# Windowed attention with a squared-ReLU layer: batch 0 started as 512 tokens, v cast by its own load, q and k ahead of v, and one transpose moved to the DMA

## The chip, the core and the metric

The kernel runs on one core of a Trainium2 chip. The metric is the device time of one execution in microseconds (us); the number given for the kernel before is the median of eight runs. The profile is of one execution. Engines: PE multiplies matrices, ACT evaluates functions, DVE and POOL work elementwise, SP only issues DMAs here. POOL issues DMAs too[...]. Each engine works through its own list of instructions in order.

## What is computed

Four batches of 768 tokens with 8 heads of 64. Each token attends to the first 4 tokens (the sinks) and to the 128 tokens up to itself; the output, one row of 512 a token, goes through two dense layers with a squared ReLU between them.

```python
scores = scale * np.matmul(q, k.transpose(0, 1, 3, 2))       # 4 x 8 x 768 x 768
keep = (pos[None, :] < 4) | ((rel >= 0) & (rel < 128))
scores = np.where(keep, scores, -1e9)
a = exp(scores - max); a = a / sum(a)
x = (a @ v), heads side by side                               # 3072 x 512
h = np.maximum(x @ w_in, 0); out = (h * h) @ w_out            # 512 -> 2048 -> 512
```

## The kernel before

**Tiling.** A batch is six tiles of 128 tokens, handled in three parts of 256 tokens, s = 0, 1, 2. Heads go in four pairs, m = 0 to 3. For one part and one pair: `scores` (L563) multiplies keys by queries into PSUM (tile `ps`), `expo` (L597) is the exponential on ACT (tile `expm`), a mask follows (`domask`, L604; in batch 0 a bias is instead added on PE by matmuls at L573 and the mask falls away), `values` (L624) multiplies by v for two pairs at a time (tile `po`), and `norm` (L648) divides on DVE into `xn_sb`. The sink keys have a small matmul of their own (`pk`) and exponential (`es`). `bridge` (L673) turns x by eight PE transposes (tile `px`), and `bridge_copy` (L684) brings it from PSUM to `xT`. For batches 2 and 3 (NATURAL) the turns of q, k and x are DMA transposes from SP instead (L434, L664). `layer1` (L691) multiplies 16 blocks of w_in by xT into `pm`, squares the ReLU with ACT and DVE; `layer2` (L722) multiplies by w_out into `py`.

**Loading.** For batches 0 and 1 q and k come as f32 (`load_qk`, L323, tile `qr`), are cast and regrouped on DVE, POOL or ACT (`regroup`, L451, tile `qs`), turned on PE (`transpose`, L468, tile `pt`) and copied from PSUM (`unload`, L486, tile `qkT`). A row that lies together in HBM is 64 f32 values times the number of tokens a partition takes: 512 B for groups of 256 tokens, 1 KB for groups of 512. v comes as f32 in rows of 256 B (`load_v`, L352, tile `vf`) and is cast by DVE or POOL (`cast`, L506). Batches 2 and 3 load q, k and v through POOL's queue, which casts (`load_natural`, L366). The weights are loaded and cast through POOL's queue too, in eight DMAs (`load_w_in`, `load_w_out`, L296 to L310).

**Order.** `Plan` (L41) is a planner that runs when the program is built: every piece of work is an `op` with a key (its wish for a place), the engines that can do it with a cost in us, what it comes after, the PSUM buffers it takes (two in the pool `att`, two in `den`), and for DMAs a queue. It always takes the op that can start first, and so fixes each engine's order. PE_SLACK (L18), the `margin` of DMAs and the fractions at L813 to L849 only steer this choice. `behind` makes a DMA's issue wait for an earlier DMA to land; `warm` (L196) puts matmuls without use into expected pauses of PE.

**The start.** The lines L784 to L811 give the order of the loads. Batch 0 is three groups of 256 tokens (L319). SP loads q and k of group 0, then half of group 1, v of part 0, the other half, v of part 1. The first w_in load waits for the k load of group 1's second half (L794); the first q k load of the last group waits for the first w_out load, and batch 1's q k for the third.

Of the kernel before, what the change touches and what calls it, by code (L numbers as in the profile page):

```python
# [17 lines left out]
PE_SLACK = 0.219  # L18
# [115 lines left out]
def kernel(  # L134
# [28 lines left out]
    sizes = dict(att=2, den=2, qr=5, qs=6, vf=3, expm=8, r=3, osb=2)  # L163
# [149 lines left out]
    qr_slot, qs_slot, vf_slot = {}, {}, {}  # L313
    qn_t, qn_slot = {}, {}
    qr_t, qs_t, vf_t, ex_t, bank_t = {}, {}, {}, {}, {}
# [3 lines left out]
    GROUPS[0] = [(0, 2), (256, 2), (512, 2)]  # L319
# [3 lines left out]
    def load_qk(b, m0, ti, g, behind=None, yields=()):  # L323


        t0, n = GROUPS[b][g]
        if b == 0 and g < 2:
            half, share = g, (b, m0, ti)
        elif n == 2:
            half, share = m0 // 2, (b, "last", ti)  # L330
        else:
            half, share = None, (b, m0, ti)
        if not half:
            qr_slot[share] = Slot("qr", 2)
        qr_slot[b, m0, ti, g] = qr_slot[share]

        def run(e):
            if half is not None:
                if half == 0:
                    qr_t[share] = work["qr"].tile([128, 2, 4, n * D], FP32, name="qr", tag="qr")  # L340
                t = qr_t[share][:, half]
            else:
                t = work["qr"].tile([128, 4, n * D], FP32, name="qr", tag="qr")
            qr_t[b, m0, ti, g] = t
            return [nc.sync.dma_start(  # L345
                out=t,
                in_=(q, k)[ti][b, 2 * m0:2 * m0 + 4, t0:t0 + 128 * n, :].rearrange(
                    "h (p t) d -> p h (t d)", t=n))]
        ops["qk", b, m0, ti, g] = dma_op("sp", ("qk", b, m0, ti, g), run, 32 * ROW[256 * n], behind,
                                         () if half else [qr_slot[share]], yields)  # L350

    def load_v(b, s, behind=None, yields=()):  # L352

        sl = vf_slot[b, s] = Slot("vf", 1)
        for i in range(2):
            t = 2 * s + i

            def run(e, i=i, t=t):
                if i == 0:
                    vf_t[b, s] = work["vf"].tile([128, 2, H, D], FP32, name="vf", tag="vf")  # L360
                return [nc.sync.dma_start(  # L361
                    out=vf_t[b, s][:, i], in_=v[b, :, 128 * t:128 * t + 128, :].rearrange("h p d -> p h d"))]
            dma_op("sp", ("v", b, t), run, 8 * 8 * ROW[256], behind if i == 0 else None,
                   [sl] if i == 0 else (), yields)

    def load_natural(b, s, older_values):  # L366

        begun = [ops["layer1", b - 2, 0, 0], w_out_op[3]]
        for ti in (1, 0):
            if s == 0:  # L370
                qn_slot[b, ti] = Slot("qr", NT)
            for i in range(2):
                t = 2 * s + i

                def run(e, t=t, ti=ti):
                    if t == 0:
                        qn_t[b, ti] = work["qr"].tile([128, NT, DM], BF16, name="qn", tag="qr")
                    return [nc.gpsimd.dma_start(  # L378
                        out=qn_t[b, ti][:, t, :].rearrange("p (h d) -> p h d", d=D),
                        in_=(q, k)[ti][b, :, 128 * t:128 * t + 128, :].rearrange("h p d -> p h d"))]  # L380
                o = dma_op("pool", ("qk", b, ti, t), run, 64 * 0.032,
                           ("v", 1, 3) if (b, ti, t) == (2, 1, 0) else None,
                           [qn_slot[b, ti]] if t == 0 else ())
                o.after += begun
                o.margin = 2.229
        for t in (2 * s, 2 * s + 1):
            def run(e, t=t):
                return [nc.gpsimd.dma_start(  # L388
                    out=v_sb[b % 2][:, t, :, 0:D],
                    in_=v[b, :, 128 * t:128 * t + 128, :].rearrange("h p d -> p h d"))]  # L390
            o = dma_op("pool", ("v", b, t), run, 64 * 0.032)
            o.after += begun + older_values
            o.margin = 2.229
# [6 lines left out]
    def attention(b, key):  # L400
# [16 lines left out]
        def stage(g, f0, f1, side):  # L417
# [9 lines left out]
            if b in NATURAL:  # L427
                for s in range(NS):
                    for ti in (1, 0):
                        for i in range(2):  # L430
# [8 lines left out]
                            ops["turn", b, ti, t].margin = 4.81  # L439
# [3 lines left out]
            for m in range(0, NP, w) if b not in NATURAL else ():  # L443
                f = 0.08 * m
                m0 = m - m % 2
                bs = Slot(side, 2)
                regs = []
                for ti in (1, 0):
                    sl = qs_slot[b, m, ti, g] = Slot("qs", 1)

                    def regroup(e, m=m, m0=m0, ti=ti):  # L451
                        t = qs_t[b, m, ti, g] = work["qs"].tile([128, w, n, 2, D], BF16, name="qs", tag="qs")
                        r = qr_t[b, m0, ti, g][:, 2 * (m - m0):2 * (m - m0) + 2 * w, :]
                        if w == 2:
                            copy(e, t, r.rearrange("p (m h) (t d) -> p m t h d", m=2, d=D))
                        else:
                            copy(e, t[:, 0], r.rearrange("p h (t d) -> p t h d", d=D))
                    who = {"pool": 0.17 + w * n * 0.11}
                    if b or g < 2:
                        who["dve"] = 0.06 + w * n * 0.094  # L460
                    if b == 0 and g == 0:
                        who["act"] = 0.2 + w * n * 0.107
                    regs.append(op(at(f), who, regroup,
                                   after=[ops["qk", b, m0, ti, g]] + prev_tr + begun, takes=[sl],
                                   reads=[qr_slot[b, m0, ti, g]]))
# [38 lines left out]

            for s in range(t0 // 256, last // 256) if b not in NATURAL else ():
                def cast(e, s=s):  # L506
                    copy(e, vb[:, 2 * s:2 * s + 2, :, 0:D], vf_t.pop((b, s)))
                ops["cast", b, s] = op(at(0.3 + 0.5 * (256 * s - t0) / (last - t0)),
                                       {"pool": 1.08, "dve": 0.75} if g < 2 else {"pool": 1.08}, cast,
                                       after=[ops["v", b, 2 * s], ops["v", b, 2 * s + 1], c_sinks] + older_values + begun,  # L510
                                       reads=[vf_slot[b, s]])


            if g == 0:
# [7 lines left out]
                def sink_values(e):  # L522
                    for j in range(NP):
# [5 lines left out]
                A["sink_values"] = op(at(0.36), {"pool": 1.4, "dve": 0.9}, sink_values,  # L529
                                      after=older_values + [c_fill, c_sinks, ops["vs_in", b]])  # L530
# [23 lines left out]
            biased = b == 0 and g < 2  # L554
            for s in range(t0 // 256, last // 256):
                fs = 0.36 + 0.5 * (256 * s - t0) / (last - t0)
                norms = []
                for m0 in (0, 2):
# [4 lines left out]
                    def scores(e, ms, s=s, m0=m0, banks=banks):  # L563
# [32 lines left out]
                    for j, m in enumerate((m0, m0 + 1)):  # L596
# [19 lines left out]
                        if biased:  # L616
                            masked.append(ex)
                            continue
                        masked.append(op(at(fm + 0.03), {"pool": 1.3, "dve": 0.7} if s else {"dve": 0.58, "pool": 1.1},
                                         domask, after=[ex, late["masks"]]))  # L620
# [40 lines left out]
                if b in NATURAL:  # L661
                    for t in (2 * s, 2 * s + 1):
# [5 lines left out]
                        o_.margin = 3.168  # L668
# [115 lines left out]
    NATURAL = (2, 3)  # L784
    load_sinks("act", 0)
    for g, m0 in ((0, 0), (0, 2), (1, 0), (1, 2)):
        for ti in (1, 0):
            load_qk(0, m0, ti, g)
        if g:
            load_v(0, m0 // 2)  # L790
    for b in range(1, B):
        load_sinks("sp", b)
    for i in range(4):
        load_w_in(i, ("qk", 0, 2, 1, 1) if i == 0 else None)  # L794
    load_w_out(0)
    load_w_out(1)
    for m0 in (0, 2):
        for ti in (1, 0):
            load_qk(0, m0, ti, 2, ("w_out", 0) if m0 == 0 and ti == 1 else None, [("w_out", 1)])
    load_v(0, 2, None, ())  # L800
    load_w_out(2, ("v", 0, 4), [("v", 0, 5)])
    load_w_out(3, None, ())
    for m0 in (0, 2):
        for ti in (1, 0):
            load_qk(1, m0, ti, 0, ("w_out", 2) if m0 == 0 and ti == 1 else None, [("w_out", 3)])
    for m0 in (0, 2):
        for ti in (1, 0):
            load_qk(1, m0, ti, 1, None, ())
    load_v(1, 0, None, ())
# [3 lines left out]
    LO, HI = 0.03, 0.504  # L813
    for b in range(B):
        if b == 0:
            at = attention(0, lambda f: f - 1.0)
            at(0, 0.0, 0.5, ("den", "att"))
            at(1, 0.5, 1.0, ("den", "att"))
            w_in_op[2].follow += [ops["cast", 0, 0]]
            w_out_op[0].follow += [ops["cast", 0, 1]]  # L820
            late["masks"] = op(-0.029, {"pool": 3.0}, build_masks, after=[c_tri, ops["bridge", 0, 1]])
            at(2, 1.0, 0.869, ("att", "den"))
# [4 lines left out]
        else:  # L827
            for i, fb in enumerate(range(0, NFB, 2)):
                layer1(b, b + 0.306 * i / 8, (fb, fb + 1), 0, 512, (0, 1))
        for i, fb in enumerate(range(0, NFB, 4)):  # L830
            if b == 0:
                layer1(b, 0.225 + 0.179 * i / 4, range(fb, fb + 4), 512, 256, (2,))
            else:
                layer1(b, b + 0.306 + 0.167 * i / 4, range(fb, fb + 4), 512, 256, (2,))
        if b + 1 < B:
# [3 lines left out]
            if b == 0:  # L839
                at = attention(1, lambda f: f)  # L840
                at(0, 0.063, 1.0, ("att", "den"))
                at(1, 0.249, 0.449, ("att", "den"))
            else:
                attention(b + 1, lambda f, b=b: b + LO + (HI - LO) * f)(0, 0.0, 1.0, "att")
        for u in range(NS):
            if b == 0 and u < 2:
                layer2(b, u, lambda i, part, u=u: 0.403 + 0.303 * (4 * part + 2 * u + i) / 24, by_part=True)
# [38 lines left out]
```

The softmax here doesn't subtract the row's maximum and nothing guards it: scores larger than these inputs give would overflow.

## Time and profile before

| | us |
|---|---|
| median of 8 runs | 226.07 (225.93 to 226.33) |
| the profiled execution | 226.17 |
| its span in the profile | 224.5 |
| first matmul of the first dense layer | 18.76 |
| PE busy | 215.7 |
| ACT busy | 115.3 |
| DVE busy | 103.5 |
| POOL busy | 63.5 |

The span is the time from the first to the last instruction; 1.67 us of the execution lie around it. The page gives the busy time of each engine, the span in 40 slices of 5.6 us, and the chain of work that ended last, followed back from the end. PE's warm-up matmuls count as busy. Up to 18.76 us PE works on batch 0's attention alone; then the dense layers of each batch run with the attention of the next between them, and the last 41 us have nothing but batch 3's dense layers.

### The profile page before, as it was taken

To read this page: it belongs to the slowest core of one execution; us is meant where nothing else is said; L and a number is where in the kernel's file an instruction comes from. 1 tells how busy PE (TensorE), PEld (TensorE's weight loads), DVE (VectorE), ACT (ScalarE), POOL (GpSimd) and SP (SyncE) were. 2 spreads that over 40 slices of the span, in tenths; PEclk is the share of its full clock that TensorE was granted. 3 is DMA by queue.
4 is the path that set the end of the run, shared out by engine and by line. 5 is a ranking of instruction groups with operands and counts; after the bars stand their busy time and mean duration, and the time that the engine had idled before them with its cause. 6 is when DMAs were issued, how large, how long until landed. Compare 5 with 4: busy or idle time off the path is not lost.

```text
span 224.5 us, 4571 instructions
## 1 busy us (share of the span) xinstructions
PE 215.7 (96%) x1919; PEld 137.9 (61%) x1941; DVE 103.5 (46%) x190; ACT 115.3 (51%) x130; POOL 63.5 (28%) x97
## 2 busy tenths in 40 slices
PE   7989999999999999999999999999999999999993
PEld 7557996457865796555454555587464555884441
DVE  7573534456775577446372533456344123440010
ACT  2486365517776587287636276665443066551010
POOL 5179016134389935987200000000002000000000
PEclk9999999999999999999999999999999999999999
DMA  5999996999999999999999552000121430000222
GB/s 168 264 192 205 213 227 148 187 354 274 214 240 160 125 204 131 163 129 200 153 129 136 147 152 58 3 0 14 36 103 26 133 120 0 0 0 3 93 95 93
DMA packets 86357, 29.70 MB, mean 132 GB/s; under 512 B 70336, under 2 KB 82880, under 8 KB 86336
## 3 DMA queue, kind: packets, MB, share of 16 engines
q0 software_dynamic: 40128, 8.92, 50.6%
q1 hardware_dynamic: 46024, 20.35, 39.6%
q8 instruction: 15, 0.25, 0.5%
q10 hardware_dynamic: 184, 0.14, 0.2%
q14 instruction: 6, 0.05, 0.1%
HBM read 27.30 MB, written 6.29 MB: 150 GB/s over the span
## 4 chain that ended last, share of the span: by engine, by line
PE 87%; DMA 5%; SPq 3%; ACT 2%; issue 1%; DVE 1%; ACTq 0%
PE pm L701 38%; PE py L741 37%; PE po L641 6%; PE ps L580 4%; DMA w_in_sb<-in_moe_w_in_dram 3%; DMA qr<-in_k_dram 2%; ACT r L710 2%; SPq L345 1%; SPq L361 1%; PE pt L477 1%; PE px L678 1%; PE pk L540 0%; DVE qkT L208 0%; ACT qkT L206 0%; DVE osb L208 0%
## 5 line engine op out<-in xcount | busy, mean ns | idle before, releaser
L701 PE MATMUL pm<-xT,w_in_sb 128*128 128x256 bf16 (+1 forms) x576 | 87.0, 308 | 1.1 <-ACT r L710 0.6
L741 PE MATMUL py<-w_out_sb,gT 128*128 128x512 bf16 x364 | 86.6, 379 | 1.2 <-issue 0.2
L701 PEld LDWEIGHTS <-w_in_sb 128*128 128x128 bf16 x576 | 62.9, 114 | 21.8 <-issue 2.1
L710 ACT ACTIVATE r<-pm 128x1024 bf16<-128x1024 f32 x48 | 49.2, 1026 | 33.7 <-PE pm L701 27.2
L741 PEld LDWEIGHTS <-gT 128*128 128x128 bf16 x384 | 35.4, 98 | 38.5 <-issue 1.4
L599 ACT ACTIVATE expm<-ps 128x1024 bf16<-128x1024 f32 (+1 forms) x48 | 43.3, 953 | 22.6 <-PE ps L580 21.4
L717 DVE TENSOR_TENSOR gT<-r 128x1024 bf16<-128x1024 bf16 x48 | 33.2, 691 | 44.5 <-ACT r L710 44.5
L608 DVE TENSOR_TENSOR expm<-expm,mask 128x1024 bf16<-128x1024 bf16 (+1 forms) x37 | 24.6, 671 | 16.6 <-ACT expm L599 16.0
L206 ACT ACTIVATE osb<-py 128x1024 f32<-128x1024 f32 x10 | 10.3, 1027 | 25.1 <-PE py L741 18.0
L222 POOL TENSOR_SCALAR_AFFINE_SELECT expm<-expm 128x512 bf16<-128x512 bf16 x4 | 2.5, 638 | 68.4 <-ACT expm L599 62.7
L641 PEld LDWEIGHTS <-expm 128*128 128x128 bf16 x352 | 16.6, 97 | 4.9 <-issue 0.8
L641 PE MATMUL po<-v,expm 128*128 128x65 bf16 x352 | 17.9, 193 | 0.3 <-DVE v L208 0.2
L653 DVE TENSOR_TENSOR xn_sb<-po,rc 128x512 bf16<-128x512 f32 x24 | 16.6, 691 | 0.8
L652 DVE RECIPROCAL rc<-po 128x8 f32<-128x8 f32 x24 | 5.0, 206 | 24.4 <-PE po L641 24.0
L580 PE MATMUL ps<-qkT 64*128 64x128 bf16 (+1 forms) x256 | 14.7, 238 | 0.4
L580 PEld LDWEIGHTS <-qkT 64*128 64x128 bf16 x256 | 8.1, 94 | 10.3 <-issue 8.9
L641 PE MATMUL po<-vs,es 128*128 128x65 bf16 x128 | 13.1, 193 | 0.0
L210 POOL CAST qs<-qr 128x512 bf16<-128x512 f32 x11 | 7.9, 732 | 18.2 <-DMA qr<-in_k_dram 11.8
L208 DVE COPY osb<-py 128x1024 f32<-128x1024 f32 (+2 forms) x3 | 2.3, 780 | 21.0 <-PE py L741 17.9
L641 PEld LDWEIGHTS <-es 128*128 128x128 bf16 x128 | 11.7, 97 | 0.0
L378 POOL DMA_DIRECT2D qn<-in_k_dram x12 | 10.8, 910 | 2.7 <-DMA vf<-in_v_dram 2.7
L388 POOL DMA_DIRECT2D v<-in_v_dram x12 | 10.7, 898 | 2.8 <-DMA qn<-in_q_dram 2.4
(51 smaller groups left out, 113.1 us busy)
## 6 DMA issues: line engine op xcount, KB each, us to landing
out_dram<-osb SPq DMA_DIRECT2D x11, 512.0 KB, 3.2
vf<-in_v_dram SPq DMA_DIRECT2D x12, 256.0 KB, 5.6
qr<-in_k_dram SPq DMA_DIRECT2D x8, 256.0 KB, 4.9
qr<-in_q_dram SPq DMA_DIRECT2D x8, 256.0 KB, 4.4
w_in_sb<-in_moe_w_in_dram POOLq DMA_DIRECT2D x4, 512.0 KB, 8.6
w_out_sb<-in_moe_w_out_dram POOLq DMA_DIRECT2D x4, 512.0 KB, 9.3
qn<-in_k_dram POOLq DMA_DIRECT2D x12, 128.0 KB, 7.4
qn<-in_q_dram POOLq DMA_DIRECT2D x12, 128.0 KB, 9.0
```

The source lines that it names most:

```text
L206: nc.scalar.activation(out=dst, in_=src, func=AF.Copy)
L378: return [nc.gpsimd.dma_start(out=qn_t[b, ti][:, t, :].rearrange("p (h d) -> p h d", d=D), in_=(q, k)[ti][b, :, 128 * t:128 * t + 128, :]. ...
L388: return [nc.gpsimd.dma_start(out=v_sb[b % 2][:, t, :, 0:D], in_=v[b, :, 128 * t:128 * t + 128, :].rearrange("h p d -> p h d"))]
L580: nc.tensor.matmul(ps[:, h2, o:o + w], lhsT=qkT_sb[r, m, 1, c, :], rhs=qkT_sb[r, m, 0, qb:qb + w // 128, :], start=(i == 0 and not biased) ...
L599: nc.scalar.activation(out=x[:, :, o:512], in_=bank_t["s", b, s, m][:, :, o:512], func=AF.Exp, scale=scale)
L608: nc.vector.tensor_mul(x[:, :, o:512], x[:, :, o:512], mk[:, :, o:512])
L641: nc.tensor.matmul(pv[:, i, h2, :], lhsT=lhsT, rhs=rhs, start=(n_ == 0), stop=(n_ == len(mms) - 1))
L653: nc.vector.tensor_tensor(out=xn_sb[:, 2 * s:2 * s + 2, 128 * m0:128 * m0 + 256].rearrange("p i (j h d) -> p j i h d", j=2, d=D), in0=pv[: ...
L701: nc.tensor.matmul(pm[:, i, :], lhsT=w_in_sb[:, fb // 4, kb, fb % 4:512:4], rhs=xT[:, c0 // 256:(c0 + cw) // 256, kb, :], start=(kb == 0), ...
L710: nc.scalar.activation(out=r, in_=bank_t.pop(tag), func=AF.Relu)
L717: (nc.vector if e == "dve" else nc.gpsimd).tensor_mul(gT_sb[c0 // 512][:, fbs[0]:fbs[0] + n, c0 % 512:c0 % 512 + cw], r, r)
L741: nc.tensor.matmul(pm[:, i, :], lhsT=gT_sb[t // 4][:, fb, 128 * (t % 4):128 * (t % 4) + 128], rhs=w_out_sb[:, fb, :], start=(fb == 0), sto ...
```

## The change

Batch 0 becomes a group of 512 tokens and one of 256, so that its first eight q k loads take one pair of heads each, in rows of 1 KB. In this first group the key copy and the query copy of a pair are two copies, and each pair's scores need both. v of batches 0 and 1 is loaded by POOL's queue straight into `v_sb`, cast on the way: the tile `vf`, the casts on DVE and POOL and SP's twelve v loads are gone. All eight q k loads of batch 0's first group stand ahead of everything else on SP; POOL issues four v loads and the sink values of batch 0 before w_in, and w_in's first load now waits for the k load of pair 2. Batch 1's q k wait for the last v load of batch 0, and batch 1's v for its own k load of pairs 2 and 3 of the last group. Part 2 of batch 1 is turned by two DMA transposes on SP (`TURNED`) instead of eight PE transposes and a PSUM copy. The fractions, margins and PE_SLACK have other values. Both parts of batch 0's first group keep the bias on PE (BIASED = 2).

```diff
-PE_SLACK = 0.219
+PE_SLACK = 0.292
...
-    sizes = dict(att=2, den=2, qr=5, qs=6, vf=3, expm=8, r=3, osb=2)
+    sizes = dict(att=2, den=2, qr=5, qs=6, expm=8, r=3, osb=2)
...
-    GROUPS[0] = [(0, 2), (256, 2), (512, 2)]
+    GROUPS[0] = [(0, 4), (512, 2)]
...
-        if b == 0 and g < 2:
-            half, share = g, (b, m0, ti)
-        elif n == 2:
+        if n == 2:
             half, share = m0 // 2, (b, "last", ti)
+        elif pairs == 1:
+            half, share = m0 % 2, (b, m0 - m0 % 2, ti)
...
             return [nc.sync.dma_start(
                 out=t,
-                in_=(q, k)[ti][b, 2 * m0:2 * m0 + 4, t0:t0 + 128 * n, :].rearrange(
+                in_=(q, k)[ti][b, 2 * m0:2 * m0 + 2 * pairs, t0:t0 + 128 * n, :].rearrange(
                     "h (p t) d -> p h (t d)", t=n))]
...
-                return [nc.sync.dma_start(
-                    out=vf_t[b, s][:, i], in_=v[b, :, 128 * t:128 * t + 128, :].rearrange("h p d -> p h d"))]
-            dma_op("sp", ("v", b, t), run, 8 * 8 * ROW[256], behind if i == 0 else None,
-                   [sl] if i == 0 else (), yields)
+                return [nc.gpsimd.dma_start(
+                    out=v_sb[b % 2][:, t, :, 0:D],
+                    in_=v[b, :, 128 * t:128 * t + 128, :].rearrange("h p d -> p h d"))]
+            o = dma_op("pool", ("v", b, t), run, 1.15, behind if t == 2 * s else None, (), yields)
+            o.after.append(c_fill)
+        ops["cast", b, s] = o
...
-                def cast(e, s=s):
-                    copy(e, vb[:, 2 * s:2 * s + 2, :, 0:D], vf_t.pop((b, s)))
...
-                A["sink_values"] = op(at(0.36), {"pool": 1.4, "dve": 0.9}, sink_values,
-                                      after=older_values + [c_fill, c_sinks, ops["vs_in", b]])
+                A["sink_values"] = op(at(0.36), {"pool": 1.9, "dve": 1.4} if b else {"pool": 1.9}, sink_values,
+                                      after=older_values + [c_fill, c_sinks, ops["vs_in", b]] +
+                                      ([ops["bridge", 0, 1]] if b == 1 else []))
...
-                if b in NATURAL:
+                if b in NATURAL or b == 1 and s in TURNED:
                     for t in (2 * s, 2 * s + 1):
                         def turn_x(e, t=t):
                             nc.sync.dma_start_transpose(out=xT[:, t // 2, :, 128 * (t % 2):128 * (t % 2) + 128],
                                                         in_=xn_sb[:, t, :])
...
-    for g, m0 in ((0, 0), (0, 2), (1, 0), (1, 2)):
+    for m in range(NP):
         for ti in (1, 0):
-            load_qk(0, m0, ti, g)
-        if g:
-            load_v(0, m0 // 2)
+            load_qk(0, m, ti, 0, 1)
     for b in range(1, B):
         load_sinks("sp", b)
+    load_v(0, 0, None)
+    load_v(0, 1)
     for i in range(4):
-        load_w_in(i, ("qk", 0, 2, 1, 1) if i == 0 else None)
+        load_w_in(i, ("qk", 0, 2, 1, 0) if i == 0 else None)
...
+    load_w_out(2, ("qk", 0, 2, 1, 1), [("qk", 0, 2, 0, 1)])
     load_v(0, 2, None, ())
-    load_w_out(2, ("v", 0, 4), [("v", 0, 5)])
     load_w_out(3, None, ())
     for m0 in (0, 2):
         for ti in (1, 0):
-            load_qk(1, m0, ti, 0, ("w_out", 2) if m0 == 0 and ti == 1 else None, [("w_out", 3)])
+            load_qk(1, m0, ti, 0, 2, ("v", 0, 5) if m0 == 0 and ti == 1 else None, [("w_out", 3)])
...
-    load_v(1, 0, None, ())
+    load_v(1, 0, ("qk", 1, 2, 1, 1), [("qk", 1, 2, 0, 1)])
...
-            at(0, 0.0, 0.5, ("den", "att"))
-            at(1, 0.5, 1.0, ("den", "att"))
-            w_in_op[2].follow += [ops["cast", 0, 0]]
-            w_out_op[0].follow += [ops["cast", 0, 1]]
-            late["masks"] = op(-0.029, {"pool": 3.0}, build_masks, after=[c_tri, ops["bridge", 0, 1]])
-            at(2, 1.0, 0.869, ("att", "den"))
+            at(0, 0.0, 1.0, ("den", "att"))
+            late["masks"] = op(0.04, {"pool": 3.0}, build_masks, after=[c_tri, ops["bridge", 0, 1]])
+            at(1, 0.928, 1.5, ("att", "den"))
...
-                at(0, 0.063, 1.0, ("att", "den"))
-                at(1, 0.249, 0.449, ("att", "den"))
+                at(0, 0.072, 0.526, ("att", "den"))
+                at(1, 0.975, 0.471, "att")
```

## The prediction

> **What bounds the kernel now.** I read the page's busy times and slices first, then the chain of waits in order of time, then busy times by window, then single waits in the timeline. The page:
>
> ```profile
> PE 215.7 (96%) x1919; PEld 137.9 (61%) x1941; DVE 103.5 (46%) x190; ACT 115.3 (51%) x130; POOL 63.5 (28%) x97
> PE   7989999999999999999999999999999999999993
> DMA  5999996999999999999999552000121430000222
> ```
>
> PE is the bound, and no change to another engine pays unless PE starts its dense work earlier or idles less. The DMA row is full over the first 30 us, so the start may still hang on loads. The chain of waits over the start says which (start, us, what):
>
> ```profile
> 7.10 5.29 DMA qr<-in_k_dram
> 12.39 0.30 issue
> 12.69 6.03 DMA w_in_sb<-in_moe_w_in_dram
> 18.72 0.05 issue
> 18.76 1.94 PE pm L701 x16
> 20.70 1.45 PE po L641 x48
> 22.15 1.75 PE pm L701 x16
> 23.90 0.45 PE px L678 x8
> 24.35 10.48 PE pm L701 x96
> ```
>
> A late k load (issued at 7.10 because SP first had to push v) lets w_in go at 12.69; w_in lands at 18.72 and PE's dense work begins. At that point batch 0's second part is not finished: 48 `po` (1.45 us) and 8 `px` (0.45) come after. The fair mark is therefore 18.76 + 1.45 + 0.45 = 20.66 us: from there on only dense work and what lies between it remain. The changed order has no dense matmul before both parts are turned; its first `pm` stands behind the second `px`. Its start X compares with 20.66.
>
> Busy time by window (us, then PE, PEld, DVE, ACT, POOL, clock, DMA share, GB/s) shows what idling is left after the start:
>
> ```profile
> 34.83:54.35 19.52, 19.10 (x178) 10.68 (x181) 10.32 (x19) 9.61 (x12) 8.19 (x13) 1.00 0.94 243
> 54.35:75.55 21.20, 20.42 (x235) 15.20 (x236) 13.02 (x23) 14.43 (x19) 15.10 (x18) 1.00 1.73 192
> 75.55:93.67 18.12, 17.80 (x216) 13.61 (x217) 12.39 (x24) 12.36 (x14) 12.10 (x17) 1.00 1.86 167
> ```
>
> PE idles 0.42, 0.78 and 0.32 us there, and some 0.5 us in all later windows: 2.0 us is all that a better order can win after the start. The timeline names the two real stalls, first dense layer waiting for its PSUM buffer:
>
> ```profile
> 59.91 1.91 PE L701 MATMUL pm<-xT,w_in_sb 128*128 128x256 bf16 x16 [0.28 <-ACT r L710]
> 62.92 1.91 PE L701 MATMUL pm<-xT,w_in_sb 128*128 128x256 bf16 x16 [0.34 <-ACT r L710]
> ```
>
> [...] 214 GB/s with 256 B rows (56 to 60 us), 272 with 512 B (2 to 4 us), 363 with 1 KB (46 to 50 us). [...] the trace has both queues at once at 69 to 72 us with a DMA share of 2.29. [...] the chain has 0.45 for 8 `px`.
>
> **Part 1, the loads of the start.** The first 256 KB k load lands 3.0 us after its issue, at 3.8, and the second 0.85 later. With 1 KB rows I take 0.78 a load (256 KB in 0.72 us at 363 GB/s, between that and 0.85): k q of pair 0 land at about 3.7 and 4.5, pair 1 at 5.3 and 6.1. POOL finishes its constants at 4.11 and then issues four v loads of 0.89 (L388). Their packets arrive from about 6 us and share with the last three q k loads. Free sharing gives pair 3's q at 9.2, strict addition (four times 0.9 us, the spacing of landings of the `qn` loads) 12.8. I take 9.9, as most of v's small packets can fit beside q k; k of pair 3 then lands at 9.0. In the kernel before the last q of this stage lands at 13.3 (issued 8.76, 4.5 to land). v itself lands by 11 to 13, needed at 13 and 17: hidden. After v POOL does the sink values (2.16 us as at 15.85 now) and issues w_in at about 9.9, against 12.69. Its 6.0 us shrink or stay: w_in lands at 15 to 16, no longer on the path.
>
> **Part 2, the front as ACT sees it.** With loads early, the front is ACT's list. Prices: 0.60 for a 512-wide `qkT` copy on ACT, 0.69 on DVE, 0.43 for a cast on DVE, 0.81 for an exponential over 768, 1.03 over 1024, 0.39 for `es`; an ACT cast is not in the trace, between 0.43 and 0.69, I take 0.62. PE runs 40 warm-up matmuls until 5.7, as now, so the first `pt` ends and ACT starts at 6.86, as now. ACT must then do, before the last exponential ends, three copies 1.80, two casts 1.24, four exponentials over 768 3.24, four over 1024 4.12, `es` 0.39: 10.8 us, to 17.7 at best. Waits inside: 0.3 for pair 3's k (9.0), 0.15 because DVE does pair 3's first copy only after two of pair 2 and one late cast, some 0.1 of handovers: 18.3. After it 24 `po` (0.73, to 19.1), DVE's reciprocal and division (0.21 + 0.69, to 20.0), 8 `px` behind 10 warm-ups (to 20.5), and the copy of the first part's `xT`, which ends about 20.6. X = 20.6, bounds 20.1 (no ACT waits) and 22 (q k at 12.8: pair 3's cast and copy 2.5 later, part of it filled by earlier exponentials). Against 20.66: **-0.06 us**. The front is not shortened, because an ACT-bound wait takes the place of the DMA-bound one and no dense matmul fills it. DVE's and POOL's saved v casts lie beside it: nothing.
>
> **Part 3, the moved transpose.** Eight PE transposes go: **-0.45 us** of PE. Their PSUM copy of 1.0 us on ACT goes too, beside PE's work. Two DMA transposes come to SP, 1.23 us each to issue (L664), 2.5 to 8.3 to land. They stand behind the turns of batch 2's last third and before batch 3's first; in PE's new list 26 us of work lie between these `po` and the first `pm` of part 2, so a landing even 10 us late is hidden. Batch 3's turns behind them wait at most for DVE's division, long before their readers.
>
> **Part 4, loads for the body.** Everything behind w_in moves forward by about 2.5 to 3 us: before, w_out's first load is issued at 17.95, lands 11.3 later, and batch 0's last q k start at 29.25. Counting forward with the same gaps, batch 0's last q k land at 31 to 34, with PE reaching their first `pt` at X + 12.1 = 32.7 (112 `pm` of 0.108); part 2's v by 40, needed at 41.7; batch 1's first q by 46, cast by 47, needed at 47.9. Each margin is 0.7 to 1.2 us. The six v loads of batch 1 cost POOL 5.3 us, against 2.1 for its casts on POOL now; they follow batch 1's q k (about 52) and land from 57, with values at 60. Batch 2's loads start near 58 rather than 62.5. So hidden, if w_in's packets start by 12.5; each us after that costs nearly one, once, as all three margins slip together.
>
> **Part 5, PE's stalls in the body.** Counting PE, ACT and DVE through 46 to 65 us in the new order with these prices, I find no wait of a first-layer matmul for its buffer: fewer `pt` sit between them, and the second layer's first accumulator is copied out by ACT 0.7 us before it is wanted. The two stalls (0.28 + 0.34) can go; bounds: all 1.5 of the three windows gained, 1.5 lost in a new order this tight. I take **-0.4**.
>
> Sum against the profiled execution: 226.17 - 0.06 - 0.45 - 0.4 = 225.26; it stands 0.10 above the median of 226.07. Forecast **225.2**.
>
> **Rivals.** (a) Slower: v in the start. The mechanism is POOL's v packets inside the q k stream. If v's packets don't fit beside them, pair 3 lands near 12 and w_in's packets start at 13 to 14. It decides from pair 3's k later than 10 us. X becomes about 21.5 and the margins of part 4 go under by about 1: 225.26 + 0.9 + 1.0 = 227.1 (226.5 to 228). For it: one queue alone already shows a DMA share of 1.24 (w_in at 20 to 24 us), so little may be free; against it: 2.29 at 69 to 72. (b) No change: the front comes a few tenths later and the new body trades its stalls for others, leaving only the transposes or less: 225.7 to 226.5, say 226.1. For it: the closest margin that I count, batch 1's first scores after DVE's last copy of their keys, is under 0.1 us, and there are 170 more groups of work that I did not count through. (c) Faster by more: ACT never waits in the front (X = 20.1) and the body loses 1 us of idling: 226.17 - 0.5 - 0.45 - 1.0 = 224.2. Against: it needs every margin. That the change doesn't do what it says is excluded: the order shows v on POOL's queue and one PSUM turn less.
>
> **How the numbers follow.** A measurement here tells 0.2% (0.45 us) from no change. Forecast (224.6 to 225.6) 0.38, (c) 0.10, (b) 0.20, (a) and other new stalls of its size 0.32. Faster 0.48, same 0.20, slower 0.32. The forecast's own range is 224.6 to 225.6; the range that leaves out no more than 2 in 10 runs from 224.3 to 227.3.
>
> **What would show it.** Right: the first `pm` at 20 to 21 us and waiting for `xT` or `px`, never for w_in; ACT busy without a gap over 0.4 us from 6.9 to 18.3; w_in's wait for a load gone from the chain; `pm` without stalls at 55 to 65. Wrong: ACT or DVE waiting for `qr` after 9.5 us; PE waiting for `qs` near 33 or 48 us, or for v at 42; any wait of `pm` for the DMA-turned `xT`.

## The result and the profile after

| | before | after |
|---|---|---|
| median, us | 226.15 (225.75 to 226.58) | 228.73 (226.91 to 230.41) |
| ratio after to before | | 1.0111, interval 1.0092 to 1.0129 |
| the profiled execution, its span | 226.17, 224.46 | 230.38, 228.7 |
| first `pm` | 18.76 (mark 20.66) | 21.57 |
| PE's last matmul | 220.81 | 224.26 |
| from there to the end of the span | 3.65 | 4.41 |

The changed kernel is slower by 2.6 us, and its executions spread over 3.5 us where the kernel before spreads over 0.8. The profiled one is among the three of twelve with a mean TensorE clock of 0.988 to 0.991; the others had 0.995 or more, so what a half clock costs in the profile is not in the median. The ratios, here and below, leave out executions that are over 1.5% above the fastest of their kernel, and the median above leaves out the profiled one.

The page of the changed kernel, busy times and two of the rows of slices:

```profile
PE 217.1 (95%) x1923; PEld 138.0 (60%) x1943; DVE 103.3 (45%) x193; ACT 115.2 (50%) x131; POOL 63.3 (28%) x97
PE   7699999999699999999999999999999999999992
...
PEclk9999999999979999999999999999999999999998
```

PE has 0.45 us of matmuls less to do, yet is busy 1.4 us longer. One slice at 57 to 63 us has a 6 in PE's row; the next one has a 7 in the clock's. Busy time by window (us, then PE, PEld, DVE, ACT, POOL, clock, DMA share, GB/s) around it:

```profile
60.00:62.90 2.90, 1.15 (x13) 0.74 (x12) 1.52 (x3) 1.43 (x3) 2.68 (x4) 1.00 2.32 151
62.90:67.10 4.20, 4.20 (x31) 3.21 (x31) 1.50 (x3) 0.64 (x1) 3.51 (x4) 0.59 2.21 213
```

PE loses 1.75 us in the first window and works at a mean clock of 0.59 in the second. The timeline of PE names the wait, and the chain of waits (start, us, what) follows it back:

```profile
60.91 0.24 PE L634 MATMUL po<-v,expm 128*128 128x65 bf16 x2
62.90 0.46 PE L634 MATMUL po<-v,expm 128*128 128x65 bf16 x10 [1.76 <-DMA v<-in_v_dram]
63.20 5.00 PE L694 MATMUL pm<-xT,w_in_sb 128*128 128x256 bf16 x29
```

```profile
46.28 0.68 DVE qs L208 x2
46.96 0.02 issue
46.98 0.37 SPq L348
47.35 0.05 issue
47.40 6.41 DMA qr<-in_k_dram
53.80 0.02 issue
53.83 0.02 POOLq L361
53.84 0.87 issue
54.71 0.95 POOL v L361
55.66 7.20 DMA v<-in_v_dram
```

Batch 1's v is late. SP's last q k loads wait for a `qr` buffer until DVE has cast it (46.96), POOL's first v load waits for the gate, the k load that lands at 53.80, then 0.87 us go by before its issue begins. The second tile of v lands at 62.86, when the first two `po` have run and PE stands. The clock is at half from 63.67 us, just after the pause, to 67.09, and 32 `pm` take 5.2 us instead of about 3.5 (estimated from 10.48 us for 96 in the kernel before). The two stalls at 59.9 and 62.9 in the kernel before are gone.

The start, in the timelines of DVE, first of the kernel before, then of the changed one:

```profile
6.34 0.43 DVE L208 CAST qs<-qr 128x512 bf16<-128x512 f32 x1 [0.39 <-DMA qr<-in_k_dram]
9.15 0.43 DVE L208 CAST qs<-qr 128x512 bf16<-128x512 f32 x1 [0.53 <-DMA qr<-in_q_dram]
```

```profile
6.16 0.43 DVE L208 CAST qs<-qr 128x512 bf16<-128x512 f32 x1 [1.44 <-DMA qr<-in_k_dram]
8.04 0.63 DVE L208 CAST qs<-qr 128x512 bf16<-128x512 f32 x1 [1.45 <-DMA qr<-in_q_dram]
```

Now DVE waits 2.9 us for the k and q of pair 1, PE waits behind it 1.68 us before it can turn pair 1's q, and the first `pm` comes at 21.57. In the kernel before the third and the fourth load landed at 6.32 and 7.27 us, here at about 6.1 and 8.02: hardly faster there, but w_in's landing at 18.72 stood after them and hid it.

Against the profiled execution of before, +4.2 us: start +0.9, wait for v +1.8, half clock +1.7, end +0.75, and about -1.0 for transposes and stalls that went.

### The profile page after: what moved, and what is told of

It reads as the page before. It is cut to its first block, busy times and chain, and to the rows that moved or that the text cites. A ratio compares the mean times of both kernels' runs of the same rounds, so it can differ in the third digit from the quotient of the medians.

```text
span 228.7 us, 4568 instructions
## 1 busy us (share of the span) xinstructions
PE 217.1 (95%) x1923; PEld 138.0 (60%) x1943; DVE 103.3 (45%) x193; ACT 115.2 (50%) x131; POOL 63.3 (28%) x97
## 4 chain that ended last, share of the span: by engine, by line
PE 81%; DMA 9%; DVE 2%; ACT 2%; SPq 2%; issue 1%; POOL 0%; DVEq 0%; POOLq 0%; ACTq 0%
PE pm L694 36%; PE py L734 32%; PE po L634 6%; PE ps L571 4%; DMA v<-in_v_dram 3%; DMA qr<-in_q_dram 3%; DMA qr<-in_k_dram 3%; SPq L348 2%; DVE qkT L208 1%; ACT r L703 1%; PE px L671 1%; PE pt L476 1%; ACT qkT L206 1%; PE ps L564 1%; PE pk L531 0%
## 5 line engine op out<-in xcount | busy, mean ns | idle before, releaser
L694 PE MATMUL pm<-xT,w_in_sb 128*128 128x256 bf16 (+1 forms) x576 | 88.7, 313 | 0.3 <-DVE xT L208 0.2
L599 DVE TENSOR_TENSOR expm<-expm,mask 128x1024 bf16<-128x1024 bf16 (+1 forms) x39 | 25.1, 649 | 18.6 <-ACT expm L590 18.0
L206 ACT ACTIVATE osb<-py 128x1024 f32<-128x1024 f32 x9 | 9.2, 1027 | 34.6 <-PE py L734 33.6
L222 POOL TENSOR_SCALAR_AFFINE_SELECT expm<-expm 128x512 bf16<-128x512 bf16 x2 | 1.2, 637 | 55.8 <-ACT expm L590 55.8
L571 PEld LDWEIGHTS <-qkT 64*128 64x128 bf16 x256 | 8.0, 94 | 10.1 <-issue 8.0
L208 DVE COPY osb<-py 128x1024 f32<-128x1024 f32 (+2 forms) x4 | 3.6, 890 | 21.3 <-PE py L734 18.2
L208 DVE CAST qs<-qr 128x512 bf16<-128x512 f32 x18 | 8.7, 493 | 7.5 <-DMA qr<-in_q_dram 4.0
L361 POOL DMA_DIRECT2D v<-in_v_dram x12 | 10.8, 918 | 2.7 <-DMA qr<-in_k_dram 2.7
L390 POOL DMA_DIRECT2D v<-in_v_dram x12 | 10.8, 911 | 2.2 <-DMA qn<-in_q_dram 2.0
```

The costliest lines, as they stand in the source:

```text
L206: nc.scalar.activation(out=dst, in_=src, func=AF.Copy)
L208: nc.vector.tensor_copy(out=dst, in_=src)
L361: return [nc.gpsimd.dma_start(out=v_sb[b % 2][:, t, :, 0:D], in_=v[b, :, 128 * t:128 * t + 128, :].rearrange("h p d -> p h d"))]
L571: nc.tensor.matmul(ps[:, h2, o:o + w], lhsT=qkT_sb[r, m, 1, c, :], rhs=qkT_sb[r, m, 0, qb:qb + w // 128, :], start=(i == 0 and not biased) ...
L599: nc.vector.tensor_mul(x[:, :, o:512], x[:, :, o:512], mk[:, :, o:512])
L694: nc.tensor.matmul(pm[:, i, :], lhsT=w_in_sb[:, fb // 4, kb, fb % 4:512:4], rhs=xT[:, c0 // 256:(c0 + cw) // 256, kb, :], start=(kb == 0), ...
```

## Experiments

In all of them, the time from the first `pm` to PE's last matmul is read beside the median, because the start varies from run to run. The kernel before has 200.15 us from its mark of 20.66, and 202.05 from its own first `pm`, with which the last three rows compare; the prediction comes to 200.15 - 0.45 - 0.4 = 199.3. There is one profile for each kernel.

| kernel | median (before, same chip) | ratio, interval | first `pm` | `pm` to last matmul | to the end |
|---|---|---|---|---|---|
| after | 228.73 (226.15) | 1.0111, 1.0092-1.0129 | 21.57 | 202.69 | 4.41 |
| v ungated | 226.71 (226.22) | 1.0024, 1.0008-1.0039 | 20.67 | 199.84 | 4.54 |
| v gated earlier | 227.26 (226.35) | 1.0038, 1.0025-1.0051 | 22.26 | 199.11 | 4.63 |
| matmuls in the pause | 228.47 (226.22) | 1.0102, 1.0080-1.0124 | 20.97 | 201.16 | 4.60 |
| v ungated, v of batch 0 behind q | one execution: 229.92 | | 21.26 | 202.37 | 4.60 |
| v ungated, turn on PE | 227.11 (226.35) | 1.0033, 1.0018-1.0049 | 21.59 | 200.24 | 3.91 |
| v ungated, SP filled, 12 | 226.39 (226.35) | 1.0002, 0.9984-1.0020 | 20.97 | 199.11 | 3.52 |
| the same, 24 | 226.41 (226.49) | 1.0003, 0.9992-1.0014 | 21.13 | 199.48 | 3.89 |
| the same, two queues | 226.54 (226.49) | 1.0009, 0.9995-1.0023 | 22.12 | 199.11 | 3.81 |
| before with the DMA turn | 232.54 (226.22) | 1.0245, 1.0183-1.0307 | 19.52 | 209.24 | 3.52 |
| the same, margin 6.5 | 232.62 (226.29) | 1.0271, 1.0234-1.0307 | 18.81 | 209.69 | 3.54 |
| the same, margin 8 | 233.94 (226.29) | 1.0334, 1.0310-1.0357 | 18.89 | 209.50 | 3.56 |

**The gate of batch 1's v.** First without it, every engine's order unchanged:

```diff
-            if behind is not None:
+            if behind is not None and name[:2] != ("v", 1):
```

> Changed kernel, but batch 1's v loads no longer wait for a k load to land; every instruction of every engine keeps its place. Theory V (the changed kernel loses its time because batch 1's v lands late: PE idles 1.8 us at 61 us and then runs 3.4 us at half clock): v is issued at about 52 right after POOL's last q cast, lands by 60, the 1.76 us wait of po and the half clock after it are gone, the time is 226.5 (226.0 to 227.0) and its runs spread less than 1 us. Theory F (the front costs it all, and the wait for v only takes up slack that PE would lose anyway): the wait goes, another takes its place, the time stays within 0.7 us of 228.7. Theory C (v issued earlier takes DMA time from batch 1's last q k): v lands no earlier than 61 and PE waits for qs or v as long as now.

PE runs through, in its timeline, at the place of the pause:

```profile
60.74 0.54 PE L634 MATMUL po<-v,expm 128*128 128x65 bf16 x12
61.12 3.11 PE L694 MATMUL pm<-xT,w_in_sb 128*128 128x256 bf16 x27
```

The clock stays at 1.00, and the median falls to 0.5 us above the kernel before; the executions spread over 1.5 us, where under 1 was expected. Then with an earlier gate:

```diff
-                    after_dma(d, loaded[behind])
+                    after_dma(d, loaded[("qk", 1, 0, 1, 1) if name[:2] == ("v", 1) else behind])
```

> The changed kernel, with batch 1's v loads gated on the first of the last four q k loads (landed at 52.1 in the changed kernel's trace) in place of the third (53.8). Theory V (PE waits at 61 us because v is issued too late): v lands 1.6 to 1.7 us earlier, the wait of po for v shrinks from 1.76 us to 0.0 to 0.2, the clock stays at 1.0 after it, and the time is that of the ungated kernel, 226.7 to 227.0. Rival (any gate, by its place in POOL's queue, makes the stall): wait over 1 us and half clock after it, 228 or more.

No pause at v again, clock 1.00; the median is 0.26 above the upper end of what was expected. The one profile has a late start (22.26); whether the median comes from that is not shown. The landing moved by more than the gate. POOL's v issues and SP's store of an output (512 KB), first the changed kernel, then this one:

```profile
54.71 4.46 POOL L361 DMA_DIRECT2D v<-in_v_dram  x5 [2.71 <-DMA qr<-in_k_dram]
...
55.19 0.39 SPq L750 DMA_DIRECT2D out_dram<-osb  x1
```

```profile
53.16 5.55 POOL L361 DMA_DIRECT2D v<-in_v_dram  x6 [1.04 <-DMA qr<-in_k_dram]
...
55.87 0.39 SPq L750 DMA_DIRECT2D out_dram<-osb  x1
```

v is issued 1.55 us earlier, but its second tile lands 4.1 us earlier (58.80 against 62.86). In the changed kernel the store is issued 0.5 us after v and its packets run from 56.1 to 58.5; the first of v come at 57.6, nearly all after 58.1. With the earlier gate v's first two tiles are issued 2.7 and 1.8 us ahead of the store and land 3.6 and 4.7 us after their own issue, against 5.1 and 7.2. The other profiles go the same way: the second tile takes 7.6 us with matmuls in the pause, where v's first issue is 0.8 us ahead of the store, 4.7 to 5.8 where it is 2.3 to 2.7 ahead, 4.8 and 4.4 where it is 3.4 and 5.1. So the loss seems to have two parts, the gate and a store that a slightly late v falls behind; the gate is shown by taking it away, the store only by these times, as no run moves it alone.

**The half clock.** 28 matmuls without use, just ahead of these `po`:

```diff
+                        for _ in range(28 if (b, s, m0) == (1, 0, 0) else 0):
+                            nc.tensor.matmul(po[:, 0, 0:128], lhsT=ident, rhs=ident, start=True, stop=True)
```

> Changed kernel with 28 matmuls without use (about 1.6 us) in the wait for batch 1's v, nothing else. Theory V with its clock part right: the wait for v stays (PE is at v's landing at the same time), but the clock stays 1.0, the 32 pm after it take 3.5 us and not 5.2, the time is 227.1 (226.5 to 227.6) with a spread under 1 us. If the half clock is not brought about by PE's pause: the pm still take 5.2 us in some runs and the time stays at 228.7 with a spread of 3 us. If the added matmuls are themselves on the path (v landing early in most runs): slower than 228.7 by up to 1.6 us.

The clock stays at 1.00 and the spread is 1 us, as expected, though of four executions only; the median does not fall to 227.1, a miss by 1.4 us:

```profile
60.33 1.74 PE L621 MATMUL po<-ident 128*128 128x128 bf16 x28
61.91 0.23 PE L636 MATMUL po<-v,expm 128*128 128x65 bf16 x2
62.44 0.46 PE L636 MATMUL po<-v,expm 128*128 128x65 bf16 x10 [0.31 <-DMA v<-in_v_dram]
```

The added matmuls stand on PE for 1.74 us and v is then still 0.31 away: the pause is only filled. What they spare, the half clock, most executions of the changed kernel did not have. So the median's loss is the wait. The three executions with a low clock are the slowest of the changed kernel (230.25 to 230.41), but the nine others still run from 226.91 to 230.13: the half clock makes only the upper end of the spread, and the rest of it is not explained. Four executions of kernels without the wait (SP filled, two queues, turn on PE) have mean clocks of 0.982 to 0.992 too, at 228.4 to 230.6 us, without a trace that could tell why.

**The start.** v of batch 0 held back behind pair 1's q (with batch 1's v ungated):

```diff
+            if name == ("v", 0, 0):
+                after_dma(ds[0], loaded["qk", 0, 1, 0, 0])
```

> As e1, and batch 0's first v load also waits for the q load of pair 1 (lands near 8), so that no v packet moves before the q k loads are nearly all done. A look at the landings only; w_in is issued later by this and the whole is slower (229 to 231). If v's packets in the q k stream were what made q k late (11.2 for the last instead of 9.9): the last q lands by 10.2, the one of pair 1 by 6.5. If the q k stream itself is slower than I took (0.9 us a load and not 0.78): pair 1's q again at 8.0, the last between 10.1 and 10.6.

In this one execution q of pair 1 landed at 7.12 us, between the two forecasts, and k of pair 3 at 9.31; the last q's cast began at 10.1, as the first forecast had it, but with v issued early it began at 10.2 in the ungated kernel. There q of pair 1 and k of pair 3 landed at 6.49 and 9.21, in the changed kernel at 8.02 and 10.22, and v's first packet came at 8.1 us, behind pair 1's q. The order of v doesn't sort these numbers, and in all three the loads from pair 2's k on follow each other by 0.72 to 0.76 us. What differs is when pair 1 comes through. The windows 3.5 to 5.5 us of the kernel before and of the changed one show the rate in the last column:

```profile
3.50:5.50 2.00, 2.00 (x21) 2.00 (x20) 1.68 (x7) 0.00 (x0) 0.62 (x3) 1.00 0.91 264
```

```profile
3.50:5.50 2.00, 2.00 (x21) 2.00 (x20) 1.01 (x4) 0.00 (x0) 2.00 (x5) 1.00 0.83 231
```

GB/s of 264 and 231, after 310 and 360 in the microsecond ahead; the ungated kernel has 299, the one gated earlier 180. The stream has a hole there, in the kernel before too. Over the seven profiles with this start the first `pm` follows the cast of pair 1's q. It begins at 6.51 us in the ungated kernel (first `pm` 20.67), at 7.31 to 7.44 in three (20.97 to 21.13), at 8.04 and 8.17 in two (21.57 and 21.59), and at 8.48 with the earlier gate (22.26).

The kernel with v held back also tells what a late w_in costs: its packets begin at 14.7 us, 2.75 later than in the ungated kernel, and PE then waits three times for `qs`, 0.57 + 1.27 + 0.59 = 2.4 us between 34 and 52 us. From the first `pm` to the last matmul it takes 2.5 us more.

Is the hole one of the queue? Three of the q loads issued by ACT (SP filled as below):

```diff
-            return [nc.sync.dma_start(
+            return [(nc.scalar if (b, g, ti) == (0, 0, 0) and m0 else nc.sync).dma_start(
```

> As the kernel with 24 filling loads, but the q loads of batch 0's first 512 tokens, pairs 1 to 3, are issued by ACT (idle until 6.9 us) and only the k loads and pair 0's q by SP. Theory Q (the first q k loads are slowed by a hole in their one queue at 3.5 to 5.5 us, which makes q of pair 1 land at 6.5 to 8.5 and the first pm of the changed order start at 20.7 to 22.3): with a second queue the hole is filled, q of pair 1 lands at 5.5 to 6.5 and the first pm starts at 20.3 to 20.7, so the time is 0.3 to 0.8 below the kernel with one queue: 225.5 to 225.9, faster than before. Rival (the hole belongs to the DMA engines or to the memory, not to the queue): q of pair 1 lands at 7 to 8.5 again, the first pm starts at 21 or later, and the time does not move or rises by 0.2 to 0.5, as q then shares with k.

DVE's wait for pair 1's k in its timeline is the longest of all, and the time is what it was:

```profile
7.83 0.96 DVE L209 CAST qs<-qr 128x512 bf16<-128x512 f32 x2 [3.00 <-DMA qr<-in_k_dram]
```

A second queue doesn't fill the hole (265 GB/s in the same window, first `pm` at 22.12), so the rival forecast is the one that came. What makes the hole stays open.

**The end.** In the trace's packet records of the changed kernel and of four of its relatives, an instruction fetch of 8192 bytes starts 1.8 to 2.3 us after PE's last matmul and takes 0.3 to 0.7 us. In all five eight of the last store's 128 packets, one sixteenth, an even share of the 16 DMA engines that the page counts, end after the fetch, at 2.5 to 3.0 us, the others by 2.3; the last of the store's sixteen completions comes 0.6 to 0.8 us after the fifteenth. In the kernel before the last fetch is 5.6 us ahead of PE's last matmul, and the completions end together, at 2.6. To move the fetch, SP gets loads that nobody reads:

```diff
+    pad = consts.tile([32, 12, 8], FP32, name="pad")
...
+            if (b, u) == (2, 2):
+                for i in range(12):
+                    nc.sync.dma_start(out=pad[:, i, :], in_=v[0, :, 0:NSINK, 0:8])
```

> The kernel with batch 1's v loads ungated, plus twelve 1 KB loads of nobody's data issued by SP just before the store of batch 2's last rows (near 180 us), when SP has nothing to do until 208. Theory T (the end of the changed kernel is later by an instruction fetch: SP's instruction stream lost about ten DMA issues, so its last 8192-byte fetch falls 1.9 us after PE's last matmul and holds up one DMA engine under the last store): the fetch moves to well before PE's end, the last PE instruction to the end of the span goes back from 4.5 to about 3.65 us, and the time is 0.85 lower than without the loads: about 225.85, ratio to the kernel before 0.998 to 0.999. Rival (the late end belongs to the last store itself or to the order of the last layer): the tail stays at 4.4 to 4.6 us and the time at about 226.7, ratio 1.002.

> The kernel with ungated v and filled SP, with 24 loads of nobody's data on SP instead of 12. Theory T (the position of SP's last instruction fetch sets the end): the fetch moves further ahead of the end, the tail stays near 3.5 us, and the median is that of the kernel with 12, 0.0 to 0.2% above or below the kernel before: 226.0 to 226.4. Rival (the shorter tail with 12 was chance): the tail returns to 4.5 us in the profile and the time to about 226.9. It is also the kernel that the next one is compared with, on the same chip.

The fetch goes from +1.93 to +1.04 us, ahead of the last store's packets, and the end is 3.52 us instead of 4.54; the median, against before on its own chip, goes from +0.5 to 0. That is about half of the 0.85 expected; with intervals of 0.3 to 0.4 us on each side the size is not settled. With 24 loads the fetch stays at +1.03 (a miss: it should have moved again), with 3.89 us to the end. Over all profiles a fetch at 1.8 us or later goes with 4.4 to 4.6 us, any other place with 3.5 to 3.9. That the fetch holds up the last store is read from the one sixteenth of its packets and from their times; how much of it is in the medians is less sure, and that it hangs on SP's own list is not shown.

**The moved transpose.** Turned back to PE in the ungated kernel, and alone in the kernel before:

```diff
-    NATURAL, TURNED, BIASED = (2, 3), (2,), 2
+    NATURAL, TURNED, BIASED = (2, 3), (), 2
```

> The kernel with batch 1's v loads ungated, and the last third of batch 1's x turned by PE again (8 px of 0.057 us and their PSUM copy on ACT). If the moved transpose is worth its PE time, this is slower than with the DMA turn by 0.45: about 227.15, ratio 1.0045. Rival (the turn is worth nothing or less, as PE's idle gaps absorb it or the DMA turn disturbs the rest): 226.7 or below, ratio 1.002 or less. SP then has two DMA turns fewer, so by theory T the last instruction fetch falls later still or drops out of the program: then the tail may be 3.6 us instead of 4.5 and the time 0.85 lower, which the trace tells apart.

From first `pm` to last matmul it is 200.24 against 199.84 us in the ungated kernel, +0.40 where 0.45 was expected. But the five profiles with the DMA's turn and no wait for v run from 199.1 to 199.8 there, so the size is known only to 0.4 to 1.1. The median is 227.11, as forecast, but by luck in part: the forecast had the end unchanged, and here the fetch falls at -5.8 us and the end is 3.91, 0.6 shorter, while the first `pm` of the profile is 0.9 later. By their medians the two kernels are the same within their intervals.

```diff
-                if b in NATURAL:
+                if b in NATURAL or b == 1 and s == 2:
```

> The kernel before with one part of the change: part 2 of batch 1 turned by two DMA transposes instead of eight PE transposes. The step of the prediction (0.45 us of PE work removed, the transposes hidden): 225.7 (225.4 to 226.0). If the DMA transposes are late for the first layer or hold SP's queue: slower than 226.15, up to 228. If the planner's new order behind it moves other waits: anything between.

A miss by 6.8 us (6.0 without the slowest of four executions). The planner fills the place of the eight `px` by drawing other work forward:

```profile
79.22 0.51 PE L678 MATMUL px<-ident,xn_sb 128*128 128x128 bf16 x6 [1.24 <-DVE xn_sb L653]
...
84.58 0.82 PE L580 MATMUL ps<-qkT 64*128 64x256 bf16 x8 [3.47 <-DMA qkT<-qn]
```

Batch 2's scores now stand ahead of the DMA that turns their keys, and the clock is at half for 6.8 us from 83.8 on. Two larger margins on those turns (`margin` 6.5 and 8 for 4.81 at L439 of before):

> The kernel before with the last third of batch 1's x turned by DMA, and 6.5 in place of 4.81 us of margin on the turns of batch 2's q k, so that batch 2's first scores are placed later in PE's order. Theory O (the loss of the first such kernel came from scores placed ahead of their keys, not from the turn itself): the wait of ps for qkT (3.47 us) and the half clock after it are gone and the 8 px of batch 1's last third are saved: 225.6 to 225.9, ratio 0.997 to 0.999, the fastest of all. Rival (the order found with any margin waits elsewhere in the body): one wait over 0.5 us between 75 and 110 us, time 226.5 or more.

> The same with 8 us of margin (the same first place of the first scores on PE 16 places earlier, the later ones otherwise spaced; with 9 and 10 the order is the same as with 8). Theory O: no wait of ps for qkT, 225.6 to 225.9. Rival: a wait over 0.5 us in the body, 226.5 or more.

The wait for `qkT` is gone in both, and with 6.5 these stand in its place:

```profile
80.03 0.23 PE L641 MATMUL po<-v,expm 128*128 128x65 bf16 x2 [0.31 <-DVE expm L608]
82.19 0.23 PE L641 MATMUL po<-v,expm 128*128 128x65 bf16 x2 [1.63 <-DVE expm L608]
84.36 0.62 PE L678 MATMUL px<-ident,xn_sb 128*128 128x128 bf16 x6 [0.38 <-DVE xn_sb L653]
86.09 2.29 PE L701 MATMUL pm<-xT,w_in_sb 128*128 128x512 bf16 x5 [1.11 <-ACT xT L206]
```

Theory O falls: it isn't one pair of scores that is placed badly. As these waits read, work is drawn together until DVE's masks, its division and ACT's copy are all behind PE, and a half clock of 6.8 us comes again. By the profiles the turn gained in the changed kernel's order; it lost with all three margins tried in the order of before; other fractions were not tried there. No version run here is faster than the kernel before; the ungated one with SP filled equals it.

## Why the prediction was wrong

The forecast was 225.2 with 0.32 for slower; it is 228.7, outside the range that was to leave out 2 in 10.

- **Part 4 failed, and decides.** "The six v loads of batch 1 ... follow batch 1's q k (about 52) and land from 57, with values at 60 ... So hidden." The k load that gates them landed at 53.80, as the load ahead of it on SP waited until 46.96 for a `qr` buffer; POOL took 0.87 us from release to issue. So v was issued at 54.71 and not at about 52, its first two tiles landed 5.1 and 7.2 us later, at 59.77 and 62.86, with a store among their packets, and the values wanted them at 60.9. PE stood 1.76 us. The chain of reasoning counted loads by their gaps in the old order but not the gate's own parts: buffer, landing, restart of POOL, what else is issued then. Taking the gate away gives back 2.0 us of the median. The list of signs had a wait for v at 42, not this one. The rest of part 4 held: PE idles 0.3 us from 21.57 to 46. Its rule that w_in's packets may start up to 12.5 and each us after costs nearly one fits the one execution with v held back (2.2 us after 12.5, 2.4 us of waits for `qs`).
- **Part 1: the term "0.78 a load" was too small.** It was taken from two loads and from the rate in the body (363 GB/s), while before's own window at 3.5 to 5.5 us has 264. Pair 1's q, put at 6.1 us, landed at 6.5 to 8.5 in the five profiles with this start that record it. Pair 3's k (9.0) landed at 9.2 to 10.6. The sign that was named, ACT or DVE waiting for `qr` after 9.5 us, is in the changed kernel's trace: 0.45 us on ACT at 10.3, 0.54 on DVE at 11.3.
- **Part 2: the ACT-bound start holds only when the loads are quick.** X = 20.6 was met in one profile (20.67); over the seven with this start it is 20.67 to 22.26, the middle one 21.13, +0.5 us on the mark. DVE and PE wait for pair 1 instead. v was no cause of that, since its first packet came after pair 1's q. So rival (a) had the sign, and with 21.5 for X nearly the start of the profile, for another reason; its mechanism, v inside the q k stream, was the author's estimate and can have touched only the loads behind pair 1. Its time, 226.5 to 228, was too low.
- **Part 3 was right in sign, by the profiles:** -0.45 forecast, -0.4 to -1.1 measured, not to be told from noise in the medians; `pm` never waited for the DMA's turn.
- **Part 5 was right:** both stalls gone. Without the wait for v, the stretch from the first `pm` on takes 199.1 to 199.8 us, forecast 199.3.
- **Not in the sum:** the end, +0.75 to +1.0 us in the profiles, which no view of before can show, since it goes with where an instruction fetch falls (1.8 us or later behind PE's last matmul: 4.4 to 4.6 us to the end, elsewhere 3.5 to 3.9).

An estimate for the median from these parts: +0.5 start, -0.7 body, +0.85 end, +1.5 to 2 for v (the pause of 1.76, the 2.0 of the ungated kernel): 2.2 to 2.7, measured 2.6. It is no independent check, as v's part rests on the medians too.

## What to carry to other kernels

A new gate on a load is dated by its whole path, not by the transfer alone: the buffer that its predecessor waits for, the landing, the restart of the issuing engine (0.87 us here), and, as it seems here, any large transfer issued close behind it (512 KB, 0.5 us). A load's price at the start is read from the start of the trace, since the body's rate was a third higher in the kernel before (363 against 264 GB/s). A list scheduler's order is part of what is measured: an edit of 0.45 us, put alone into another order, cost about 6 us.

## What the runs showed of the hardware

- After PE's pause of 1.76 us the clock was at 0.5 for 3.41 us, from 0.8 us behind its end; in the kernels of 232 us, with more or longer pauses close together (1.24 and 3.47 us; 1.63 and 1.11 with margin 6.5), for 6.83, twice as long. Two more of the twelve executions of the changed kernel had mean clocks as low, 0.991 and 0.988 against 0.990. Pauses of 1.68 us near 9 us in the changed kernel and of 1.41 with the earlier gate were followed by no half clock (1.00 in both).
- POOL's casting v load of batch 1 needed 2.9 us from the start of its issue to its first packet when a store of 512 KB was issued 0.5 us after it; the store's packets came first, 0.9 us after its issue. In seven other kernels of this order, with the store 0.8 us behind or more, it was 1.7 to 1.9 us.
- POOL's issue began 0.9 us after the landing that it waited for, in all three traces with a gate (changed, gated earlier, matmuls in the pause).
- In the start single packets of 1 KB took up to 0.7 to 2.0 us, by kernel, in the nine that start with 1 KB rows (median 0.046); with 512 B rows, in the kernel before and its three relatives, the longest up to 9 us took 0.16 to 0.74.
